# Sparse attention, soft mixture of experts and a gated feed-forward on one core: the order of the late expert weight loads

## The chip, the core and the metric

The kernel runs on one core of a Trainium2 chip. The metric is the time on the device in microseconds, from one launch. The arithmetic is done in float32, on TensorE (PE) in several passes; VectorE (DVE), ScalarE (ACT) and GpSimd (POOL) do the rest, and SyncE (SP) issues nearly all DMAs.

## What is computed

Three layers follow each other. First attention with 4 batches, 8 heads, 576 positions and 64 features a head; half the heads see the last 32 positions, half every 32nd position. Its output, 2304 tokens of 512, goes through a soft mixture of 8 experts with 4 slots each, and that through a gated feed-forward with 1536 hidden features.

```python
scores = scale * q @ k.T                      # masked: local for heads 0-3, strided for 4-7
x = softmax(scores) @ v                       # -> [2304, 512]
logits = x @ phi                              # [2304, 32]
d = softmax(logits, axis=0);  c = softmax(logits, axis=1)
slot_input = (d.T @ x).reshape(8, 4, 512)
for e in range(8):                            # w1[e] 512x1024, w2[e] 1024x512
    slot_out[e] = relu(slot_input[e] @ w1[e]) @ w2[e]
x = c @ slot_out.reshape(32, 512)
out = (silu(x @ w_gate) * (x @ w_val)) @ w_out
```

## The kernel before

**Stages.** A loop over 16 units (a pair of batches and a head) does the attention: scores (`qk`), exponentials (`expo`), transposes (`tr`) and the product with the values (`pv`). Beside it the outputs of pairs of heads (`x` tiles, six buffers of one tag) are transposed into `xT` (one buffer), multiplied with phi (`logits`, line 354), and summed into the expert slots (`slot`, line 421) with the transposed exponentials `eT`. After the last unit the softmax over tokens is finished (`weights_a`, `weights_b`, `slot_in`), and the slots' inputs stand in `sz`. Then the first expert product runs over 16 weights of one megabyte (`w1_mm`, line 623, in the order of `W1ORDER`: 1 to 6, 0, 7, 14, 8, 15, 9, 10, 13, 12, 11), then the second over another 16, numbered 16 to 31 (line 712, in the order of `W2ORDER`: the even ones, then the odd ones), and then the feed-forward, whose weights are converted on the chip tile by tile; its output products (line 819) fill the second half of the time.

**Expert weights and their memory.** SP loads the weights in halves of 512 KB; `loads` is the list of (weight, half) in the order of issue, and `load_half(k)` issues the next k of them. The order is written out by hand and interleaved with the units by `WSCHED`. SP is one queue that works in order: an issue whose memory is still in use holds up all that stand behind it. Fifteen buffers of two halves (pool `wp`) are filled during the attention, three of them first with feed-forward weights (`PRE`), whose memory 16, 18 and 20 take over once they are converted. 22, 24 and 26 have buffers of their own (pool `wp2`, with `sz` beside them) in the memory of the pool `ld`, where keys, values and masks lie; it is closed in step 16, after the last `pv`. Weights 0, 14 and 15 (`SPEC`) lie in the memory of attention outputs: their halves are called `wx` and take five of the six `x` buffers in turn, as their last readers (the `slot` matmuls) are done, and one half takes `xT`, whose last readers are the last `logits` matmuls. Weight 13 (`SPLIT`) has one half in the exponentials' tile `tmp` and one in `eT`. 28 and what follows take the buffers of weights 1 to 10 as `w1_mm` lets them go; each `w1_mm` of a weight that is not one of the four special ones calls `load_half(2)`.

**The order before.** After 20 the list reads: (0,0), 22, 24, 26 (six halves), (13,0), (0,1), (14,0), (14,1), (15,0), (15,1), (13,1), 28 and on. Half (0,0) is issued in step 15 or 16 by the `+ 1` of lines 605 and 613, into the `x` buffer that the `slot` call of step 18 (first batch pair, second output) reads last. (0,1) goes into `xT`.

Of the kernel before, what the change touches and what calls it, by code (L numbers as in the profile page):

```python
# [9 lines left out]
F32 = mybir.dt.float32  # L10
# [16 lines left out]
NB = 15  # L27
NB2 = 3
SPEC = (0, 14, 15)
W2ORDER = tuple(range(16, 32, 2)) + tuple(range(17, 32, 2))  # L30
SPLIT = 13
WORDER = list(range(1, 13)) + list(W2ORDER[:6]) + list(SPEC) + [SPLIT] + list(W2ORDER[6:])
W1ORDER = (1, 2, 3, 4, 5, 6, 0, 7, 14, 8, 15, 9, 10, 13, 12, 11)
PRE = [("g", 0), ("g", 1), ("o", 0)]
# [23 lines left out]
WSCHED = [2] + [2] * 16  # L58
# [53 lines left out]
def build(ctx: ExitStack, tc: tile.TileContext, cst, phi, kq, vh, w1, w2, wgv, wo, out):  # L112
# [13 lines left out]
    ap_ = es_att.enter_context(tc.tile_pool(name="att", bufs=1))  # L126
# [24 lines left out]

    wsrc = [w1[j] for j in range(16)] + [w2[j] for j in range(16)]
    loads = [(j, hf) for j in PRE + WORDER for hf in range(2)]
    loads.remove((SPEC[0], 0))
    loads.insert(2 * (NB + len(PRE)), (SPEC[0], 0))
    loads.remove((SPLIT, 0))
    loads.insert(2 * (NB + len(PRE) + NB2) + 1, (SPLIT, 0))
    wt, gt = {}, {}
    wn = [0]
    NW = len(loads)  # L160

    def load_half(k, pool=wp, bufs=NB):
        for _ in range(k):
            if wn[0] >= NW:
                return
            j, hf = loads[wn[0]]
            if j in SPEC:
                wt[j, hf] = (ap_.tile([128, 1024], F32, tag="xT", name="wx", bufs=1) if hf and j == SPEC[0] else
                             ap_.tile([128, 1024], F32, tag="x", name="wx", bufs=6))
            elif j == SPLIT:  # L170
                wt[j, hf] = ap_.tile([128, 1024], F32, tag="eT", name="wx", bufs=1) if hf else tmp[:, 0:1024]
            elif hf == 0:
                a = pool.tile([128, 2048], F32, tag="w", name="w", bufs=bufs)
                if j in PRE:
                    gt[j] = a.bitcast(I32)
                wt[j, 0], wt[j, 1] = a[:, 0:1024], a[:, 1024:2048]
            if j in PRE:
                o, i = wt[j, hf].bitcast(I32), (wgv if j[0] == "g" else wo)[j[1], hf].bitcast(I32)
            else:
                o, i = wt[j, hf], wsrc[j][hf]  # L180
            SP.dma_start(out=o, in_=i)
            wn[0] += 1
# [65 lines left out]
    def load_qk(u):  # L248
        if u >= 16:
            return  # L250
        SP.dma_start(out=kt[u % NQK][:, PAD:], in_=kq[u])

    def load_v(u):
        if u >= 16:
            return
        t = vt[u % NV]
        SP.dma_start(out=t[W - 64:W], in_=vh[u])
        t4 = t.rearrange("p (b i d) -> p b i d", b=2, i=NT)
        for i0, i1 in ((1, 3), (3, 6), (6, 9)):
            POOL.tensor_copy(t4[0:W - 64, :, i0:i1, :], t4[64:W, :, i0 - 1:i1 - 1, :])  # L260
# [10 lines left out]
    def qk(u):  # L271
        y = UNITS[u][1] // 4
        e = etile(u)
        q, k = qbd[u % NQK], kt[u % NQK]
        mx = mxs[u] = ap_.tile([128, NT], F32, tag="mx", name="mx", bufs=2)
        for i0, i1 in zip(CUT, CUT[1:]):
            ps = bank("sc", 2)
            for i in range(i0, i1):
                c0 = 64 * i
                for b in range(2):  # L280
                    h = slice(64 * b, 64 * b + 64)
                    PE.matmul(out=ps[h, W * (i - i0):W * (i - i0) + W], lhsT=q[h, 64 * i:64 * i + 64],  # L282
                              rhs=k[h, c0:c0 + W], start=True, stop=True, skip_group_check=True)
            p3 = ps[:, 0:(i1 - i0) * W].rearrange("p (j k) -> p j k", k=W)
            m3 = ms[:, i0:i1] if y else ml[:, i0:i1] if i0 == 0 else ml[:, 1:1 + i1 - i0]
            DVE.scalar_tensor_tensor(out=e[:, i0:i1], in0=p3, scalar=0.125, in1=m3, op0=ALU.mult, op1=ALU.add)  # L286
            DVE.tensor_reduce(out=mx[:, i0:i1], in_=e[:, i0:i1], axis=AX, op=ALU.max, negate=True)  # L287

    def expo(u, k):
        e, mx = etile(u), mxs[u]  # L290
        for i in range(CUT[k], CUT[k + 1]):
            ACT.activation(out=e[:, i], in_=e[:, i], func=AF.Exp, scale=1.0, bias=mx[:, i:i + 1])  # L292

    def tr(u):
        e = etile(u)
        for t in range(3):
            ps = bank("tr", 3)
            for j in range(3):
                PE.transpose(ps[0:W, 128 * j:128 * j + 128], e[:, 3 * t + j], ident)  # L299
            ACT.copy(attile[0:W, 3 * t:3 * t + 3], ps[0:W, 0:384].rearrange("p (j q) -> p j q", j=3))  # L300

    def pv(u):
        bp, h = UNITS[u]
        y = h // 4
        st, e = divmod(h % 4, 2)
        if e == 0:
            xt[bp, y, st] = ap_.tile([128, NT, 128], F32, tag="x", name="x", bufs=6)
        x, v = xt[bp, y, st], vt[u % NV]
        dn = ap_.tile([128, 2, NT, 1], F32, tag="dn", name="dn", bufs=2)
        half = []  # L310
        for i0, i1 in zip(CUT, CUT[1:]):
            ps = bank("pv", 2)
            for i in range(i0, i1):
                for b in range(2):
                    PE.matmul(out=ps[64 * b:64 * b + 64, 65 * (i - i0):65 * (i - i0) + 65], lhsT=attile[0:W, i, 64 * b:64 * b + 64],  # L315
                              rhs=v[0:W, 65 * (NT * b + i):65 * (NT * b + i) + 65], start=True, stop=True, skip_group_check=True)
            p3 = ps[:, 0:65 * (i1 - i0)].rearrange("p (j d) -> p j d", d=65)
            DVE.tensor_scalar_add(dn[:, 0, i0:i1], p3[:, :, HD:HD + 1], 1.0e-9)
            half.append((i0, i1, p3))
        DVE.reciprocal(dn[:, 1], dn[:, 0])  # L320
        for i0, i1, p3 in half:
            DVE.tensor_tensor(out=x[:, i0:i1, 64 * e:64 * e + 64], in0=p3[:, :, 0:HD],
                              in1=dn[:, 1, i0:i1].to_broadcast([128, i1 - i0, HD]), op=ALU.mult)

    xT = {}
# [167 lines left out]
    with tc.manual_schedule():  # L493
# [11 lines left out]
        load_qk(1)  # L505
        SP.dma_start(out=phi_t, in_=phi.rearrange("p (c s) -> p c s", c=4))
        load_half(WSCHED[0])
        load_v(1)
        load_qk(2)
# [43 lines left out]
        for p in range(8):  # L553
            bp, y, st = p // 4, p % 2, p // 2 % 2
            n = 2 * p + 3
# [30 lines left out]
        n = 0  # L586
        while n < 16 or any(k >= n for k in late):
            if n < 16:
                qk(n)
                load_qk(n + NQK)  # L590
            if 0 <= n - 1 < 16:
                tr(n - 1)
            if n < 16:
                expo(n, 0)
            for fn, a in side.pop(n, []):
                fn(*a)
            if n < 16:
                expo(n, 1)
            for fn, a in mid_.pop(n, []):
                fn(*a)  # L600
            if 0 <= n - 1 < 16:
                pv(n - 1)
                load_v(n + 1)
                if n == 16:
                    load_half(2 * (NB + len(PRE)) + 1 - wn[0])
                    es_ld.close()
                    wp2 = es_w2.enter_context(tc.tile_pool(name="wp2", bufs=NB2, side="right",
                                                           reuse_waits="tile"))
                    load_half(2 * NB2, wp2, NB2)
                    szt.append(wp2.tile([128, 4, 288], F32, name="sz", bufs=1))  # L610
                    POOL.memset(szt[0], 0.0)
            if n < 16:
                load_half(min(WSCHED[n + 1], 2 * (NB + (len(PRE) if n > 13 else 0)) + (n > 14) - wn[0]))
            for fn, a in late.pop(n, []) + first_.pop(n, []):
                fn(*a)
            n += 1
# [92 lines left out]
        for n, j in enumerate(W2ORDER):  # L709
            e, hf = divmod(j - 16, 2)  # L710
# [269 lines left out]
```

## Time and profile before

| | us |
|---|---|
| median of 3 runs | 359.76 |
| the 3 runs | 358.86, 359.76, 360.13 |
| the profiled execution | 358.82 |
| its span, first to last instruction | 356.9 |

| engine | busy us | share of the span | instructions |
|---|---|---|---|
| PE, matmuls | 337.2 | 94% | 2860 |
| PE, weight loads | 247.3 | 69% | 2860 |
| DVE | 236.4 | 66% | 485 |
| ACT | 194.7 | 55% | 462 |
| POOL | 140.9 | 39% | 147 |

Busy time of PE is that of pipelined matmuls, so 94% does not say that it runs at its peak. "SPq", "PEq" and the like are an engine's sequencer: waits and issues, in which the engine itself does nothing. "PEld" is the loading of the stationary operand. An arrow out<-in names the tile written and the tile or tensor read, L181 is line 181 of the kernel, and a name behind an arrow in brackets is what ended the idle time before. The attention takes the time up to about 100 us, the expert products that from 108 to 147 us, the feed-forward the rest.

### The profile page before, as it was taken

To read this page: it belongs to the slowest core of one execution; us is meant where nothing else is said; L and a number is where in the kernel's file an instruction comes from. 1 tells how busy PE (TensorE), PEld (TensorE's weight loads), DVE (VectorE), ACT (ScalarE), POOL (GpSimd) and SP (SyncE) were. 2 spreads that over 40 slices of the span, in tenths; PEclk is the share of its full clock that TensorE was granted. 3 is DMA by queue.
4 is the path that set the end of the run, shared out by engine and by line. 5 is a ranking of instruction groups with operands and counts; after the bars stand their busy time and mean duration, and the time that the engine had idled before them with its cause. 6 is when DMAs were issued, how large, how long until landed. Compare 5 with 4: busy or idle time off the path is not lost.

```text
span 356.9 us, 7428 instructions
## 1 busy us (share of the span) xinstructions
PE 337.2 (94%) x2860; PEld 247.3 (69%) x2860; DVE 236.4 (66%) x485; ACT 194.7 (55%) x462; POOL 140.9 (39%) x147
## 2 busy tenths in 40 slices
PE   8999998998799999979998999999998999999995
PEld 4788887897574243347785766876776788888885
DVE  4999889788360054396987998999778824252442
ACT  1997988978430023347766556456456445353441
POOL 2233323212100200226575768438368654334431
PEclk9999999999999999978999999999999999999999
DMA  7999999966679999933332433333300003030331
GB/s 288 409 407 407 391 378 388 376 220 242 241 290 416 408 411 406 409 139 115 118 119 85 150 119 118 118 120 118 118 1 2 1 0 119 0 118 2 119 116 62
DMA packets 20804, 71.94 MB, mean 202 GB/s; under 512 B 2336, under 2 KB 2720, under 8 KB 20768
## 3 DMA queue, kind: packets, MB, share of 16 engines
q1 hardware_dynamic: 20624, 71.45, 52.8%
q8 instruction: 23, 0.38, 0.4%
q14 instruction: 13, 0.11, 0.1%
q10 hardware_dynamic: 144, 0.01, 0.0%
HBM read 66.73 MB, written 4.72 MB: 200 GB/s over the span
## 4 chain that ended last, share of the span: by engine, by line
PE 53%; DVE 16%; DMA 12%; ACT 7%; POOL 6%; issue 5%; DVEq 0%; POOLq 0%; ACTq 0%
PE o L819 31%; DMA w<-in_w 9%; ACT tmp L292 4%; DMA wx<-in_w 3%; PE gv L792 3%; PE pv L315 3%; PE sc L282 3%; PE gv L793 3%; POOL hl L801 2%; DVE mx L287 2%; PE tr L299 2%; POOL wol L763 2%; DVE h L799 2%; DVE tmp L286 2%; DVE wg L224 2%
## 5 line engine op out<-in xcount | busy, mean ns | idle before, releaser
L801 POOL TENSOR_TENSOR hl<-h,hh 128x512 fp32r<-128x512 f32 (+1 forms) x60 | 72.2, 1205 | 90.7 <-ACT hh L800 90.6
L819 PE MATMUL o<-woh,hh 128*128 128x512 f32 (+1 forms) x222 | 86.8, 392 | 0.2 <-DVE acc L844 0.2
L819 PE MATMUL o<-wol,hh 128*128 128x512 f32 (+1 forms) x222 | 86.0, 390 | 0.0
L799 DVE TENSOR_TENSOR h<-gv,sg 128x512 f32<-128x512 f32 (+1 forms) x59 | 37.5, 636 | 55.7 <-ACT sg L798 42.4
L819 PE MATMUL o<-woh,hl 128*128 128x512 f32 (+1 forms) x222 | 66.7, 390 | 0.6 <-POOL hl L801 0.4
L800 ACT CAST hh<-h 128x512 fp32r<-128x512 f32 (+1 forms) x60 | 34.7, 578 | 54.8 <-DVE h L799 54.8
L819 PEld LDWEIGHTS o<-woh,hh 128*128 128x128 f32 x222 | 42.3, 190 | 10.0 <-DVE acc L844 0.6
L819 PEld LDWEIGHTS o<-woh,hl 128*128 128x128 f32 x222 | 41.8, 190 | 10.4 <-POOL hl L801 1.9
L260 POOL COPY v<-v 32x390 f32<-32x390 f32 (+1 forms) x48 | 23.9, 530 | 61.4 <-DMA v<-in_vh 52.0
L819 PEld LDWEIGHTS o<-wol,hh 128*128 128x128 f32 x222 | 42.3, 191 | 8.4
L292 ACT ACTIVATE tmp<-tmp,mx 128x96 f32<-128x96 f32 x144 | 40.0, 362 | 10.0 <-DVE mx L287 9.9
L798 ACT ACTIVATE sg<-gv 128x512 f32<-128x512 f32 (+1 forms) x60 | 33.4, 557 | 20.2 <-PE gv L792 19.3
L282 PE MATMUL sc<-k 64*64 64x96 f32 x576 | 27.8, 246 | 0.4 <-issue 0.2
L792 PE MATMUL gv<-cs,St 128*128 128x512 f32 (+1 forms) x60 | 25.7, 429 | 1.9 <-DVE St L781 1.9
L282 PEld LDWEIGHTS sc<-k 64*64 64x64 f32 x576 | 24.4, 133 | 3.0 <-issue 1.7
L763 POOL TENSOR_TENSOR wol<-wo,woh 128x512 fp32r<-128x512 f32 x12 | 15.3, 1289 | 23.3 <-ACT woh L760 23.3
L315 PEld LDWEIGHTS pv<-v,tmp 96*64 96x64 f32 x576 | 19.3, 137 | 6.4 <-ACT tmp L300 6.1
L315 PE MATMUL pv<-v,tmp 96*64 96x65 f32 x576 | 21.3, 225 | 1.9 <-ACT tmp L300 1.8
L300 ACT COPY tmp<-tr 96x384 f32<-96x384 f32 x48 | 19.7, 477 | 4.9 <-PE tr L299 4.8
L793 PE MATMUL gv<-cs,St 128*128 128x512 f32 (+1 forms) x59 | 22.4, 379 | 0.0
L299 PE MATMUL tr<-cst_t,tmp 128*96 128x128 f32 x144 | 19.9, 280 | 2.3 <-ACT xT L334 2.2
L220 DVE SCALAR_TENSOR_TENSOR cv<-g,cv 128x512 int32<-128x512 int32 x30 | 20.8, 693 | 0.6
(159 smaller groups left out, 484.9 us busy)
## 6 DMA issues: line engine op xcount, KB each, us to landing
w<-in_w SPq DMA_DIRECT2D x56, 512.0 KB, 7.7
g<-in_wgv SPq DMA_DIRECT2D x10, 1024.0 KB, 4.9
k<-in_kq SPq DMA_DIRECT2D x16, 576.0 KB, 7.5
g<-in_wo SPq DMA_DIRECT2D x5, 1024.0 KB, 4.8
v<-in_vh SPq DMA_DIRECT2D x16, 292.5 KB, 5.5
out<-osb SPq DMA_DIRECT2D x17, 256.0 KB, 2.1
wx<-in_w SPq DMA_DIRECT2D x7, 512.0 KB, 10.1
w<-in_wgv SPq DMA_DIRECT2D x4, 512.0 KB, 7.0
```

Source lines behind the costliest of these rows:

```text
L260: POOL.tensor_copy(t4[0:W - 64, :, i0:i1, :], t4[64:W, :, i0 - 1:i1 - 1, :])
L282: PE.matmul(out=ps[h, W * (i - i0):W * (i - i0) + W], lhsT=q[h, 64 * i:64 * i + 64], rhs=k[h, c0:c0 + W], start=True, stop=True, skip_grou ...
L292: ACT.activation(out=e[:, i], in_=e[:, i], func=AF.Exp, scale=1.0, bias=mx[:, i:i + 1])
L299: PE.transpose(ps[0:W, 128 * j:128 * j + 128], e[:, 3 * t + j], ident)
L315: PE.matmul(out=ps[64 * b:64 * b + 64, 65 * (i - i0):65 * (i - i0) + 65], lhsT=attile[0:W, i, 64 * b:64 * b + 64], rhs=v[0:W, 65 * (NT * b ...
L792: PE.matmul(out=pg[:, 0:n], lhsT=St[f][:, 0:128], rhs=csf[:, t0:t0 + n], start=True, stop=True)
L793: PE.matmul(out=pvv[:, 0:n], lhsT=St[f][:, 128:256], rhs=csf[:, t0:t0 + n], start=True, stop=True)
L798: ACT.activation(out=sg[:, 0:n], in_=pg[:, 0:n], func=AF.Silu)
L799: DVE.tensor_tensor(out=h[:, 0:n], in0=pvv[:, 0:n], in1=sg[:, 0:n], op=ALU.mult)
L800: ACT.copy(hh[bi, f][:, 0:n], h[:, 0:n])
L801: POOL.tensor_tensor(out=hl[bi, f][:, 0:n], in0=h[:, 0:n], in1=hh[bi, f][:, 0:n].bitcast(F32), op=ALU.subtract)
L819: PE.matmul(out=o[:, 0:c], lhsT=(a, a, l)[i][:, 128 * t:128 * t + 128], rhs=(woh, wol, woh)[i][f][:, c * k:c * k + c], start=(first and i ...
```

## The change

In the list of loads (0,0) is no longer moved ahead of 22; it stays ahead of (0,1), behind (13,0). The list after 20 then reads: 22, 24, 26 (six halves), (13,0), (0,0), (0,1), (14,0), (14,1), (15,0), (15,1), (13,1), 28 and on. (0,0) goes into `xT` and (0,1) into the `x` buffer, the other way round than before. Two counts of `load_half` lose the one half that was issued ahead. The other calls keep their counts, so that from (13,0) on each call reaches one half less far in the list; (13,1) is issued by the first `w1_mm`.

```diff
     loads = [(j, hf) for j in PRE + WORDER for hf in range(2)]
-    loads.remove((SPEC[0], 0))
-    loads.insert(2 * (NB + len(PRE)), (SPEC[0], 0))
     loads.remove((SPLIT, 0))
-    loads.insert(2 * (NB + len(PRE) + NB2) + 1, (SPLIT, 0))
+    loads.insert(2 * (NB + len(PRE) + NB2), (SPLIT, 0))
@@
-                wt[j, hf] = (ap_.tile([128, 1024], F32, tag="xT", name="wx", bufs=1) if hf and j == SPEC[0] else
+                wt[j, hf] = (ap_.tile([128, 1024], F32, tag="xT", name="wx", bufs=1) if not hf and j == SPEC[0] else
                              ap_.tile([128, 1024], F32, tag="x", name="wx", bufs=6))
@@
                 if n == 16:
-                    load_half(2 * (NB + len(PRE)) + 1 - wn[0])
+                    load_half(2 * (NB + len(PRE)) - wn[0])
                     es_ld.close()
@@
             if n < 16:
-                load_half(min(WSCHED[n + 1], 2 * (NB + (len(PRE) if n > 13 else 0)) + (n > 14) - wn[0]))
+                load_half(min(WSCHED[n + 1], 2 * (NB + (len(PRE) if n > 13 else 0)) - wn[0]))
```

## Rows read from the trace of the kernel before

**Rows 1.** The page's 40 slices of 8.9 us: granted clock, bytes moved.

```profile
PEclk9999999999999999978999999999999999999999
GB/s 288 409 407 407 391 378 388 376 220 242 241 290 416 408 411 406 409 139 115 118 119 85 150 119 118 118 120 118 118 1 2 1 0 119 0 118 2 119 116 62
```

**Rows 2.** Chain that ended last, in order of time, 86 to 162: start, us, what.

```profile
103.69 11.67 DMA wx<-in_w
...
125.58 10.38 DMA w<-in_w
...
135.97 10.23 DMA w<-in_w
...
146.25 1.08 PE pv L712 x4
```

**Rows 3.** Timeline of SP, 83 to 112: start, us, engine, line, operation, count.

```profile
83.73 7.50 SPq L181 DMA_DIRECT2D w<-in_w  x6
98.77 0.33 SPq L181 DMA_DIRECT2D wx<-in_w  x1
99.14 2.97 SPq L181 DMA_DIRECT2D w<-in_w  x6
...
103.09 7.62 SPq L181 DMA_DIRECT2D wx<-in_w  x6
```

**Rows 4.** Waits of SP, 91.5 to 99.1: total us, times, longest.

```profile
SPq L181 <- PE tr L421: 7.5, 1, 7.5
```

**Rows 5.** Line 181, the two issues at 90.42 and 90.79: time to landing.

```profile
DMA to landing us min/median/max: 4.6/5.9/7.1
```

**Rows 6.** Line 181, the one issue at 98.77: time to landing.

```profile
DMA to landing us min/median/max: 3.5/3.5/3.5
```

**Rows 7.** Busy us by stretch: PE, PEld, DVE, ACT, POOL, clock, DMA share, GB/s.

```profile
90.00:92.00 2.00, 2.00 (x29) 1.17 (x29) 0.36 (x1) 1.66 (x5) 0.00 (x0) 1.00 1.01 377
...
96.00:98.00 2.00, 2.00 (x32) 1.54 (x32) 0.92 (x4) 0.23 (x1) 0.00 (x0) 1.00 0.04 10
...
102.00:104.00 2.00, 2.00 (x33) 1.77 (x34) 1.43 (x6) 0.88 (x3) 0.00 (x0) 1.00 0.92 309
...
112.00:116.00 4.00, 4.00 (x40) 1.41 (x31) 0.00 (x0) 0.00 (x0) 0.00 (x0) 1.00 1.02 414
```

**Rows 8.** Timeline of PE's weight loads, 107 to 150: idle before and releaser in brackets.

```profile
116.68 0.12 PEld L623 LDWEIGHTS sc<-wx,sz 128*32 128x32 f32 x3 [1.14 <-DMA wx<-in_w]
...
119.26 0.12 PEld L623 LDWEIGHTS sc<-wx,sz 128*32 128x32 f32 x3 [1.16 <-DMA wx<-in_w]
...
130.51 0.13 PEld L712 LDWEIGHTS pv<-w,hz 128*32 128x32 f32 x4 [0.30 <-issue]
...
143.68 0.14 PEld L712 LDWEIGHTS pv<-w,hz 128*32 128x32 f32 x4 [0.51 <-DMA w<-in_w]
144.96 0.14 PEld L712 LDWEIGHTS pv<-w,hz 128*32 128x32 f32 x4 [1.13 <-DMA w<-in_w]
146.24 0.14 PEld L712 LDWEIGHTS pv<-w,hz 128*32 128x32 f32 x4 [1.14 <-DMA w<-in_w]
```

**Rows 9.** Timeline of POOL, 80 to 150.

```profile
93.03 1.06 POOL L611 MEMSET sz<- 128x1152 f32 x1 [5.20 <-PE pv L315]
```

**Rows 10.** Timeline of PE's matmuls, 76 to 160.

```profile
95.56 1.06 PE L354 MATMUL lg<-xT,phi_t 128*32 128x288 f32 x8 [0.35 <-ACT xT L334]
...
108.49 5.69 PE L623 MATMUL sc<-w,sz 128*32 128x512 f32 x47
```

**Rows 11.** Line 653, the one issue at 137.31: time to landing.

```profile
DMA to landing us min/median/max: 11.5/11.5/11.5
```

**Rows 12.** Timeline of ACT, 104 to 166.

```profile
150.29 1.25 ACT L198 ACTIVATE wg<-g 128x512 f32<-128x512 f32 x2
```

**Rows 13.** Busy us by stretch, columns as in rows 7.

```profile
152.00:156.00 4.00, 2.07 (x8) 1.04 (x7) 3.81 (x7) 1.07 (x3) 0.00 (x0) 0.97 0.69 271
156.00:160.00 4.00, 3.87 (x8) 2.19 (x8) 3.39 (x7) 2.23 (x4) 2.42 (x2) 0.50 0.00 0
```

## What the change does to the time: the prediction

> **What bounds the kernel now.** I read the slices first. The weight loads run at over 400 GB/s for long stretches, but between slices 8 and 11 the rate falls to 220 to 290 GB/s, before it is over 400 again [rows 1]. The question is whether that hole costs anything, so the chain of waits comes next. From 103.7 us to 146.2 us it holds DMAs alone: one expert half after another, each 10.2 to 11.7 us from issue to landing, and only then the last four matmuls of the second expert product (line 712) at 146.25 [rows 2]. So the end of the expert stage is set by when the last weight half lands, and that goes back to when the queue was fed.
>
> The timeline of SP shows where it was not fed. Six halves are issued from 83.73 on and the last of them is out at 91.23 (83.73 + 7.50). The next issue is at 98.77 [rows 3]. In between SP stands for 7.5 us in one wait, which PE's line 421 ends, the token-slot matmuls of the first batch pair [rows 4]. By the kernel's list of loads this is half (0,0): it goes into the third buffer of attention outputs, and those matmuls are its last reader. Behind it stand the six halves of 22, 24 and 26, which have nothing to do with that buffer. The DMA engines drain what is queued and then idle: 377 GB/s in 90 to 92 us, 10 GB/s in 96 to 98, 309 still in 102 to 104, then 414 [rows 7].
>
> The rest of the question is who would notice earlier weights. PE's weight loads tell it: a group of four column matmuls follows the next with 0.30 us of idle on that unit when nothing is late, and five groups have more, put down to DMA: 1.14 and 1.16 us in the first expert product, 0.51, 1.13 and 1.14 us in the second [rows 8]. Everywhere else PE runs through at its own pace, although the chain says DMA; most of the wait in the chain is beside PE work. So what earlier loads can return is bounded by these five waits.
>
> **The change, part by part.** No DMA, matmul or byte is added or taken away: 34 halves from 22's first to 31's last are issued in another order, and the two halves of weight 0 swap memory, the first into the transposed activations' tile (xT), the second into the buffer of outputs. Instruction counts on every engine stay. SP's own cost is 0.33 to 0.50 us an issue: 2.97 us for six [rows 3], unchanged.
>
> *The moved halves on SP.* After 91.23 comes 22. Its memory, and 24's and 26's, is that of the keys, values and masks. The trace has an operation with the same release: the memset of sz, in the same pool beside them, starts at 93.03, let go by PE's line 315, the last product with the values [rows 9]. So even if all six halves wait for all of that memory they leave from 93.0 on; if each waits for its own part alone, from 91.3. I take 91.3 to 93.0; neither end matters, since the halves issued at 90.4 and 90.8 land only 4.6 and 7.1 us after issue, at 95.1 and 97.9 [rows 5], so that the engines still have work, and a half into an empty queue needs 3.5 us from issue to landing [rows 6].
>
> *What is queued behind, and its waits.* Half (13,0) needs the exponentials' tile, read before that line-315 product. (0,0) now waits for xT, whose last readers are the logits matmuls, 95.56 + 1.06 = 96.6 us [rows 10]. (0,1) and (14,0) wait for what (0,0) waits for now, 98.77 [rows 3]. (14,1) follows the release that starts the chain at 103.69 [rows 2]. (15,1) and (13,1) wait for the last slot matmuls and 28 for the first expert matmuls, which start at 108.49 [rows 10]; at 0.43 us a group of four (0.13 of load and 0.30 idle [rows 8]) and two groups a weight, the first is read by about 109.4. None of these uncovers the engines: a half is 0.524 MB, at 414 GB/s [rows 7] 1.27 us, and ten halves are issuable by 99.2, so they carry the engines from 95.1 or 97.9 to 107.8 or 110.6. At 103.7 two more are let go, at about 107.7 another two, and 28 would have to land at 95.1 + 16 x 1.28 = 115.6 or later: from 109.4 it has over 6 us, with 3.5 needed [rows 6].
>
> *When the last half lands.* One hop of the chain is eight halves, in 10.23 us, or 1.28 us each [rows 2]. From the landing of the half before 22: early end, it lands 1.28 after 95.1 as the rate asks, 96.4 + 34 x 1.28 = 139.9; late end, 97.9 + 43.5 = 141.4, and with the 1.7 us that the present stretch loses on the same pace (the half of 98.77 lands at 102.3 [rows 3, 6], 33 halves later it is 146.2 and not 144.5) 143.1. Now it is 135.97 + 10.23 = 146.2 [rows 2]. The queue gains 3.1 to 6.3 us; I take 5, between the ends, since the loss of 1.7 came with the restart, which is gone.
>
> *What PE makes of it.* The five waits above, less 0.30 each: 0.84 + 0.86 + 0.21 + 0.83 + 0.84 = 3.58 us [rows 8]. The first two belong to weights 14 and 15, which would be wanted at 116.68 - 0.84 = 115.8 and at 119.26 - 0.84 - 0.86 = 117.6; they would land by 112.0 and 114.5 in the later case (11 and 13 halves after 97.9). The last three need 31's second half by 146.24 - 3.58 = 142.7. At 139.9 or 141.4 it is there; at 143.1 it is 0.4 late. So the return is 3.2 to 3.6 us, I take 3.6, and 1.4 us of the 5 is lost beside PE. Past 142.7 each microsecond of lateness is one microsecond of the result.
>
> *What comes after.* The second product's result, the softmax pieces and the memset of hz hang on PE's own progress here and move with it. The last stage reads its first converted tile from a load behind the weights: issued at 137.31, landed 11.5 us later at 148.8, first read by ACT at 150.29 [rows 11, 12]. It follows the weights on SP and comes forward by the same 3 to 6 us, so it stays ahead of a reader that comes forward by 3.6. From there the kernel is PE work of fixed size: its end comes forward whole. Nothing in the attention part ahead of 91 us is touched.
>
> A rule of the Trainium skill speaks against this much: "DMA: Bandwidth & Descriptors", section Specifications, gives an HBM limit of about 358 GB/s for a core. As an estimate, by that 34 halves would take 49.8 us and the last would land at 146.2 to 147.7, no earlier than now, and the time would stay. The trace disagrees: 414 GB/s in the stretch itself [rows 7]; I weigh slower supply below by rows alone.
>
> **The sum.** The profiled execution took 358.82 us, with a span of 356.9 and 1.9 around it. 358.82 - 3.6 = 355.2. It is 0.94 under the median of the three runs, 359.76; the same step from the median gives 356.1, which is the forecast.
>
> **The rivals.** *Supply too slow.* If the halves come at 377 GB/s, the rate of 90 to 92 us [rows 7], a half takes 1.39 us and 34 take 47.3: the last lands at 143.7 to 145.2, and PE is 1.0 to 2.5 us late on it. The gain is 1.1 to 2.6, the time 357.2 to 358.7; I put it at 357.7. For it speaks that the stretch of 100 to 107 is slow now; against it that 108 to 146 is not.
>
> *The change does not do what it says.* 22 could find a wait as long as the old one (a release of the whole pool that is tied to something near 98.8). The time stays at 359.8. Against it stands the memset at 93.03 [rows 9].
>
> *The clock spares the start of the last stage.* The granted clock is 0.50 in 156 to 160 us [rows 13], the lower level of 1.2 GHz, after 4 us in which PE was busy for 2.07; the slices show 7 and 8 tenths there [rows 1], 2 to 3 tenths and 1 to 2 tenths of 8.9 us lost, 2.7 to 4.5 us of full-clock time. Part of that is idle anyway. If earlier, denser work keeps the clock up, 1 to 3 us more come back: 353.1 to 355.1, say 354.1. Against it: the idle time before the fall lies behind the weights and moves with them, unchanged.
>
> *Slower: the clock falls again.* The same fall once or twice more on the matmuls of line 819, which have no slack, costs 2.7 to 4.5 us each. It decides against the change once more than 3.6 + 1.1 = 4.7 us are lost, so with two falls: 356.1 + 5.4 to 9 = 361.5 to 365. The place would be just behind the present fall, where PE still waits for tiles that are converted. For it speaks only that one fall is there already. The Trainium skill ("TensorE: Matmul & The Clock Gate", section "What's actually happening") says that the throttled state is the default and activity releases it; by that rule fewer waits of PE make a further fall less likely. No row shows a second one.
>
> **How the numbers follow.** Forecast 0.66 (355.5 to 356.8 with the term's ends and the runs' spread), slow supply 0.13, clock spared 0.08, no effect 0.08, slower 0.05. 0.3%, about what a measurement of this kernel can tell from no change, is 1.1 us. Faster by more: 0.66 + 0.13 + 0.08, less a little of the slow-supply end, 0.86; within: 0.09; slower: 0.05. The range takes in the spared clock's middle and slow supply's: 353.9 to 358.1, and leaves out about 0.17.
>
> **What would show each step.** SP's wait on line 421 gone or under 3 us, and 22's halves issued by 94; no slice window with 10 GB/s in 94 to 100 us; last expert half landed by 143; no idle above 0.5 us put down to DMA on PE's weight loads in lines 623 and 712; the first expert matmul still near 108.5, the second product's end near 143.7 and everything behind it shifted alike, half clock included. The prediction is wrong if 22 still waits, if the first expert matmul moves, or if the stage behind 150 us does not shift with the weights.

## The result: 355.5 us after 359.8, and the profile after

| | before | after |
|---|---|---|
| median of 7 runs, us | 359.76 | 355.52 |
| lowest and highest, us | 357.46, 362.15 | 353.83, 356.55 |
| the profiled execution, us | 358.82 | 356.04 |
| its span, us | 356.9 | 354.3 |

The ratio is 0.988, with a 95% interval from 0.984 to 0.992: 4.2 us less, 2.8 to 5.7 by the interval. The forecast was 356.1.

The slices of the page after, granted clock and bytes moved:

```profile
PEclk9999999899999999969999999999999999999999
GB/s 287 408 409 401 385 397 393 361 189 221 355 409 410 407 411 407 386 71 82 118 120 118 118 120 126 111 123 116 118 1 2 1 0 120 0 118 2 120 118 61
```

And its chain of waits, shares of the span by engine, first before and then after:

```profile
PE 53%; DVE 16%; DMA 12%; ACT 7%; POOL 6%; issue 5%; DVEq 0%; POOLq 0%; ACTq 0%
```

```profile
PE 67%; DVE 14%; POOL 6%; ACT 5%; issue 5%; DMA 2%; DVEq 0%; POOLq 0%; ACTq 0%; SPq 0%
```

The hole of the transfers is two slices long instead of four: 355 and 409 GB/s in slices 10 and 11, counted from 0, where there were 241 and 290 [rows 1]. The other two, slices 8 and 9 (71 to 89 us), lie ahead of SP's 7.5 us wait and are as low as before, 189 and 221; the prediction read all four as one hole, but the change touches the second half of it alone. DMA has 2% of the chain where it had 12%. SP's timeline (start, us, operation, count):

```profile
85.26 12.90 SPq L179 DMA_DIRECT2D w<-in_w  x12
98.26 0.38 SPq L179 DMA_DIRECT2D tmp<-in_w  x1
99.34 10.74 SPq L179 DMA_DIRECT2D wx<-in_w  x7
```

Its waits from 91 to 107 us (total, times, longest):

```profile
SPq L179 <- DVE wo L222: 3.8, 1, 3.8
SPq L179 <- DMA w<-in_w: 3.3, 4, 0.9
SPq L179 <- PE pv L419: 2.6, 1, 2.6
SPq L179 <- PE pv L313: 0.8, 1, 0.8
```

Twelve halves now leave in one run instead of six [rows 3], and no wait of 7.5 us stands among them [rows 4]. The one of 3.8 us, for feed-forward weights to be converted, is ahead of the six moved halves; the kernel before has it too, with 4.1 us. The transfers answer in the same stretches as in rows 7 (the columns are those too):

```profile
96.00:98.00 2.00, 1.65 (x15) 0.81 (x13) 0.00 (x0) 1.25 (x3) 0.00 (x0) 1.00 0.93 344
...
102.00:104.00 2.00, 2.00 (x23) 1.32 (x23) 1.63 (x5) 1.32 (x5) 0.00 (x0) 1.00 1.03 420
```

344 GB/s instead of 10, and 420 instead of 309. In the chain of waits, in order of time, nearly all is PE's own work up to 137.3 us, where DMAs stood from 103.7 to 146.2 [rows 2], and behind it stands one DMA that loads for the feed-forward:

```profile
110.11 14.30 PE sc L621 x127
...
129.92 7.00 PE pv L710 x64
...
137.42 8.32 DMA g<-in_wgv
...
145.79 2.50 POOL wol L761 x2
```

The same step of POOL in the chain before:

```profile
148.32 2.49 POOL wol L763 x2
```

That DMA is the 2%, and it sets nothing. The chain names it as what let POOL go at 145.79, 0.55 us behind the load with which the next step begins (145.24, below). In the kernel before POOL starts the same 0.55 us behind that load (148.32 - 147.77), let go by ACT; and in the run below without weight 31, where the first load for the feed-forward lands at 141.5 (136.27 + 5.2), it is 0.55 us again (145.08 - 144.53).

And on PE's weight loads the late groups of rows 8 are gone; the last of both products, and the load with which the next step begins:

```profile
110.04 0.14 PEld L621 LDWEIGHTS sc<-w,sz 128*32 128x32 f32 x4
...
142.82 0.16 PEld L710 LDWEIGHTS pv<-w,hz 128*32 128x32 f32 x8
143.28 0.13 PEld L710 LDWEIGHTS pv<-w,hz 128*32 128x32 f32 x4 [0.30 <-issue]
143.70 0.13 PEld L710 LDWEIGHTS pv<-w,hz 128*32 128x32 f32 x4 [0.30 <-issue]
...
145.24 0.98 PEld L733 LDWEIGHTS sc<-cst_t,so 128*128 128x128 f32 x8 [0.24 <-ACT so L724]
```

Where there were 1.13 and 1.14 us of idle "put down to DMA" there are now 0.30 us of the ordinary pace.

For what follows I use one length, which I call the expert stage: from the first weight load of the first product to the load with which the step behind the second begins. After, that is 145.24 - 110.04 = 35.20 us. In the kernel before the first product starts at 108.48 (its first matmul is 108.49 [rows 10]) and the step behind it here:

```profile
147.77 0.98 PEld L735 LDWEIGHTS sc<-cst_t,so 128*128 128x128 f32 x8 [0.22 <-ACT so L726]
```

That is 39.29 us. The stage is 4.1 us shorter, about as much as the medians differ. The two spans differ by 2.6 only, because the attention of the profiled execution after took 1.6 us longer; that is not the change, as the last section shows.

### The profile page after: what moved, and what is told of

It is laid out like the page before. It is cut to its first block, busy times and chain, and to the rows that moved or that the text cites. A ratio compares the mean times of both kernels' runs of the same rounds, so it can differ in the third digit from the quotient of the medians.

```text
span 354.3 us, 7429 instructions
## 1 busy us (share of the span) xinstructions
PE 335.5 (95%) x2860; PEld 250.0 (71%) x2860; DVE 236.4 (67%) x485; ACT 195.4 (55%) x462; POOL 140.2 (40%) x147
## 4 chain that ended last, share of the span: by engine, by line
PE 67%; DVE 14%; POOL 6%; ACT 5%; issue 5%; DMA 2%; DVEq 0%; POOLq 0%; ACTq 0%; SPq 0%
PE o L817 32%; PE sc L621 4%; PE pv L313 4%; PE sc L280 4%; PE gv L790 3%; PE tr L297 3%; PE pv L710 3%; PE gv L791 3%; POOL hl L799 2%; DMA g<-in_wgv 2%; ACT tmp L290 2%; POOL wol L761 2%; DVE h L797 2%; PE tr L489 2%; PE tr L331 2%
## 5 line engine op out<-in xcount | busy, mean ns | idle before, releaser
L280 PE MATMUL sc<-k 64*64 64x96 f32 x576 | 28.7, 251 | 0.7 <-issue 0.5
L280 PEld LDWEIGHTS sc<-k 64*64 64x64 f32 x576 | 25.4, 137 | 3.8 <-issue 1.6
```

## The experiments

The theory: SP's stand at one half (the 7.5 us in which it waits and issues nothing) held back six others that wait for nothing; the transfers made good for it only at the end of the second product, and PE waited for them. With the stand filled PE itself sets the end of the stage, so more transfer time buys nothing further. Rivals: the two swapped places give the gain; the transfers still set the end; the clock gives it. The stage is read from one profile of each run, the ratio from all its executions.

| run | ratio to before, 95% interval | expert stage in its profile, us |
|---|---|---|
| before | 1 | 39.29 |
| changed kernel | 0.988 (0.984 to 0.992) | 35.20 |
| changed kernel again | 0.986 (0.983 to 0.989) | 35.19 |
| order alone | 0.984 (0.981 to 0.988) | 35.19 |
| places alone | 0.999 (0.996 to 1.001) | 40.23 |
| two halves ahead | 0.992 (0.989 to 0.995) | 36.77 |
| four halves ahead | 0.990 (0.987 to 0.994) | 35.63 |
| changed, weight 31 not loaded | 0.989 (0.985 to 0.993) | 35.20 |
| before, weight 31 not loaded | 0.995 (0.992 to 0.998) | 37.69 |

**Order alone.** The changed kernel with the old places of weight 0's two halves.

```diff
+    i0 = loads.index((SPEC[0], 0))
+    loads[i0], loads[i0 + 1] = loads[i0 + 1], loads[i0]
@@
-    wt[j, hf] = (... tag="xT" ... if not hf and j == SPEC[0] else
+    wt[j, hf] = (... tag="xT" ... if hf and j == SPEC[0] else
```

> The changed order with the old places: 22, 24, 26 are issued ahead of both halves of weight 0, but its second half still lies in xT and its first in the output buffer, so the list runs (13,0), (0,1), (0,0). Theory (the gain is SP's 7.5 us stand that no longer holds back the six halves): ratio to before 0.988 to 0.990, like the changed kernel, the six halves issued by about 94 to 98, no weight-load wait for DMA in the first and second expert product. Rival (the swap of the two places gives the gain, or a part of it): ratio nearer to 1.

Measured: 0.984, and the changed kernel's stage. The ratio is a little better than forecast, but its interval reaches to 0.988 and overlaps the changed kernel's. SP's timeline has the run of twelve:

```profile
84.24 11.86 SPq L181 DMA_DIRECT2D w<-in_w  x12
```

The chain of waits, in order of time, is PE's own pace through both products:

```profile
109.07 14.30 PE sc L623 x127
...
141.85 1.90 PE pv L712 x16
```

**Places alone.** The kernel before with the halves' roles exchanged: the second half of weight 0 in the output buffer and ahead of 22, the first in xT.

```diff
-    loads.remove((SPEC[0], 0))
-    loads.insert(2 * (NB + len(PRE)), (SPEC[0], 0))
+    loads.remove((SPEC[0], 1))
+    loads.insert(2 * (NB + len(PRE)), (SPEC[0], 1))
@@
-    wt[j, hf] = (... tag="xT" ... if hf and j == SPEC[0] else
+    wt[j, hf] = (... tag="xT" ... if not hf and j == SPEC[0] else
```

> The old order with the new places: the second half of weight 0 goes into the output buffer and stands ahead of 22, as the first half did; the first half goes into xT. Theory: SP again stands some 7.5 us at that half, ratio 0.997 to 1.003, five late groups of weight loads as before. Rival (the places matter): ratio 0.988 to 0.993.

Measured: 0.999, no change. SP's timeline has the old stand:

```profile
84.60 7.49 SPq L181 DMA_DIRECT2D w<-in_w  x6
99.64 0.33 SPq L181 DMA_DIRECT2D wx<-in_w  x1
```

Its wait from 91 to 110 us:

```profile
SPq L181 <- PE tr L421: 7.5, 1, 7.5
```

And PE's weight loads are late at the end of the second product, as before:

```profile
146.79 0.14 PEld L712 LDWEIGHTS pv<-w,hz 128*32 128x32 f32 x4 [1.14 <-DMA w<-in_w]
148.06 0.14 PEld L712 LDWEIGHTS pv<-w,hz 128*32 128x32 f32 x4 [1.12 <-DMA w<-in_w]
```

The profiled execution is the slowest of its twelve (361.01 us), and its stage is 0.9 us longer than before, which the median does not show. A wait for weight 0's first half, which is issued behind the stand here, comes on top in its first product, so the late groups are six and not the expected five:

```profile
116.11 0.16 PEld L623 LDWEIGHTS sc<-wx,sz 128*32 128x32 f32 x8 [1.87 <-DMA wx<-in_w]
```

The two together settle it: the order is the whole gain. The swap of memory adds nothing that shows, since the order alone has the same stage without it.

**Two halves ahead.** The kernel before with (0,0) behind 22 instead of ahead of it.

```diff
-    loads.insert(2 * (NB + len(PRE)), (SPEC[0], 0))
+    loads.insert(2 * (NB + len(PRE)) + 2, (SPEC[0], 0))
@@
-    load_half(2 * (NB + len(PRE)) + 1 - wn[0])
+    load_half(2 * (NB + len(PRE)) - wn[0])
@@
-    load_half(2 * NB2, wp2, NB2)
+    load_half(2 * NB2 + 1, wp2, NB2)
@@
-    load_half(min(WSCHED[n + 1], 2 * (NB + (len(PRE) if n > 13 else 0)) + (n > 14) - wn[0]))
+    load_half(min(WSCHED[n + 1], 2 * (NB + (len(PRE) if n > 13 else 0)) - wn[0]))
```

> The kernel before with only the two halves of 22 ahead of (0,0), 24 and 26 behind it as before. Theory: the queue gains 2 x 1.28 = 2.6 us of work for its stand, so the last half lands some 2.6 us earlier than 146.2 for the same start of the first product; PE's wait falls by about that, of 4.1 to about 1.5 us: ratio 0.992 to 0.994. Rival (transfers start late in any case and only the whole reordering helps): ratio 1. Rival (the gain of the changed kernel lies in the clock, not in the loads): ratio without relation to the number of halves.

Measured: 0.992, and a stage of 36.77 us, 1.6 above the changed kernel's where 1.5 were expected. SP still stands, but behind eight halves, as its timeline has it:

```profile
85.25 8.44 SPq L181 DMA_DIRECT2D w<-in_w  x8
100.28 0.33 SPq L181 DMA_DIRECT2D wx<-in_w  x1
```

Two groups of weight loads are late where there were five:

```profile
143.96 0.14 PEld L712 LDWEIGHTS pv<-w,hz 128*32 128x32 f32 x4 [1.02 <-DMA w<-in_w]
145.25 0.14 PEld L712 LDWEIGHTS pv<-w,hz 128*32 128x32 f32 x4 [1.15 <-DMA w<-in_w]
```

**Four halves ahead.** The same with (0,0) behind 24 (+ 4 in place of + 2).

> The kernel before with the halves of 22 and 24 ahead of (0,0), 26 behind it. Theory: 5.1 us more work for the stand; the last half lands about 141 to 143 for a start of the first product at 108.5, PE's five waits for DMA are gone or under 0.5 us in all, and the ratio is that of the changed kernel, 0.986 to 0.989: the step from two halves to four gives the rest, and the step from four to six nothing. Rival (each half ahead gives its share, because the transfers still set the end): ratio 0.990 to 0.992 here, with a rest that only six halves give.

Measured: 0.990, in the rival's range, with an interval that reaches into the theory's, so the time does not decide. The profile says more: the stage is 35.63 us, 0.4 above the changed kernel's. SP's timeline:

```profile
83.40 10.23 SPq L181 DMA_DIRECT2D w<-in_w  x10
```

PE's last weight loads; the group before the last is split in two:

```profile
141.40 0.12 PEld L712 LDWEIGHTS pv<-w,hz 128*32 128x32 f32 x2 [0.30 <-issue]
141.82 0.12 PEld L712 LDWEIGHTS pv<-w,hz 128*32 128x32 f32 x2 [0.31 <-issue]
142.27 0.14 PEld L712 LDWEIGHTS pv<-w,hz 128*32 128x32 f32 x4 [0.33 <-DMA w<-in_w]
```

The idle of 0.33 us hides the wait. Where nothing is late four loads go at once, then the next four 0.42 us later (143.28 and 143.70 in the changed kernel). Here two go, then two, and the last four at 142.27, just behind the landing of weight 31's second half (issued at 132.03, landed 10.2 us later, at 142.2). That is one step of 0.42 to 0.45 us more, which is what the stage is longer by. So with four halves ahead the transfers still set the end, by 0.4 us, as the rival had it; only with six does PE.

The first two halves take 2.5 us off the stage, the next two 1.1, the last two 0.4. The last half lands 37.7, 35.2, 34.1 and 32.9 us after the stage's start with none, two, four and six halves ahead, so only the first pair brings about the 2.6 us that a pair was priced at, the others 1.1 each, and of the last 1.1 PE had 0.4 to take. Neither expectation has this: the rival's equal shares are not there, and "nothing" for the last pair was too strong.

**Weight 31 not loaded, in the changed kernel and in the one before.** The two halves are left out of the list, and the last four matmuls of the second product read weight 29 again: PE does the same work, one megabyte less is moved.

```diff
+    loads = [(j, hf) for j, hf in loads if j != W2ORDER[-1]]
@@
-    rhs=wch(j, k)
+    rhs=wch(j if n < 15 else W2ORDER[-2], k)
```

> The changed kernel without the load of weight 31; its matmuls read weight 29 instead, so one megabyte less is loaded and PE's work is the same. Theory (PE sets the end of the expert products now): ratio like the changed kernel's, within 0.002. Rival (the transfers still set it): 2.6 us faster than the changed kernel, ratio 0.979 to 0.981.

> The kernel before without the load of weight 31; its matmuls read weight 29 instead. Theory (in the kernel before the transfers set the end of the second product, while the two waits in the first product stay): the last two of the three late groups of the second product come on time, 1.7 us less, ratio 0.994 to 0.9965, and the two late groups of the first product stay. Rival (the loads did not hold the kernel before, the clock did): ratio 1.

Measured: in the changed kernel 0.989, no better than with weight 31 loaded, with an interval that leaves out the rival's 0.979 to 0.981, and a stage of 35.20 us, the same to the hundredth. Its chain goes through PE to the end:

```profile
142.18 1.90 PE pv L711 x16
```

SP's timeline has its last expert weights out by 129.1 (124.98 + 4.12), where the changed kernel issues the last one at 132.77:

```profile
124.98 4.12 SPq L180 DMA_DIRECT2D w<-in_w  x4
```

In the kernel before it is 0.995, and the stage falls by 1.6 us (1.7 expected): the two late groups of the first product stay (with one more of 0.61 us of idle in this execution), the last two of the second are gone. PE's weight loads:

```profile
117.38 0.12 PEld L624 LDWEIGHTS sc<-wx,sz 128*32 128x32 f32 x3 [1.15 <-DMA wx<-in_w]
119.94 0.12 PEld L624 LDWEIGHTS sc<-wx,sz 128*32 128x32 f32 x3 [1.14 <-DMA wx<-in_w]
...
144.21 0.14 PEld L713 LDWEIGHTS pv<-w,hz 128*32 128x32 f32 x6 [0.35 <-DMA w<-in_w]
```

So a megabyte less is worth 1.6 us where transfers set the end and nothing where PE does. That the changed kernel's stage is not set by its last loads is shown by this pair, not argued; no other late group is left on its weight loads.

The third rival, the clock, has no part in the stage: its granted share is 1.00 from 108 to 148 us before and from 110 to 146 us after.

**The changed kernel again**, beside the others:

> The changed kernel once more, beside the others on the same chip. Theory: ratio 0.988 to 0.990. Between profiles the start of the first expert product may differ with the granted clock in the attention; from that start to the end of the second product 34.6 us, as in the changed kernel, where before had 38.8.

Measured: 0.986, with a stage of 35.19 us. To the end of the product's last matmul it is 34.7 us (140.69 + 1.92 - 107.91), where 34.6 was expected.

## Why the prediction was right, step by step

*The stand and its end* came as forecast. 22 was put between 91.3 and 93.0; its halves left at 92.9 and 93.3, in an execution whose attention ran 1.6 us late, so at the early end: each weight waits for its own part of the old memory. 24 has the wait of 0.8 us on the last product with the values (line 313 after).

*The new waits* are there and cost nothing: 2.6 us before (14,1) and 2.8 before (15,1), between the issues at 106.1 and 109.3. The transfers kept their rate behind them, 420 GB/s in 102 to 104.

*The last half* was to land 3.1 to 6.3 us earlier, 5 as the value taken. It is issued at 132.77 and lands 10.2 us later, 32.9 us after the stage's start; before that was 146.2 - 108.5 = 37.7. That is 4.8.

*PE's five waits* were to give 3.58 us and gave 4.1. The first product's length, up to the load of the step behind it (line 696, at 124.55 before; line 694, at 124.34 after), went from 16.07 to 14.30, 1.77 where the terms made 1.70. The second half of the stage went from 23.22 to 20.90, 2.3 where they made 1.88. The mis-sized term is the third, 0.51 - 0.30 = 0.21 us. The 0.30 is the pace between groups that follow matmuls of their own kind; this group comes right behind transposes, and there the loads of two groups run together, as the row of 142.82 after shows (eight in 0.16 us). So all of 143.68 - 143.03 = 0.65 us was wait, 0.44 more than the term, of the missing 0.5. The row of 143.03 in the timeline before, which has four loads where after has eight:

```profile
143.03 0.14 PEld L712 LDWEIGHTS pv<-w,hz 128*32 128x32 f32 x4
```

*The margin* behind it is thinner than forecast: of the 4.8 us by which the last half lands earlier 4.1 return, so 0.7 are unused, where the prediction had 1.4. With four halves ahead instead of six it is used up: the last half lands 1.1 us later there, and the stage is 0.4 longer.

*The start* moved, which the prediction had named as a sign against it: the first expert matmul was to stay near 108.5 and stood at 110.0 in the profiled execution. In the second profile of the same kernel it stood at 107.9. What moved it lies ahead of every load that changed places: the run of weight loads starts at 85.26 where it started at 83.73 [rows 3], so 1.5 of the 1.6 us were lost by then, and the last section shows where.

*What comes behind* moved whole. From the stage's end to the end of the program it was 209.2 us before and 209.0 after. One reason given was wrong: the first load for the feed-forward was to come forward with the weights by 3 to 6 us. It waits for memory that PE lets go, in each of the six profiles with two halves or more moved ahead 26.94 us after the stage's start; here it left at 136.98, no more than 0.3 us earlier on the clock of the trace and 1.9 earlier against the stage's start. It lands sooner all the same, since less stands in the queue ahead of it, 8.5 us after issue instead of 11.5 [rows 11], at 145.5 (5.2 us after issue where weight 31 is not loaded). Its time to landing in the changed kernel (line 651, the issue at 136.98):

```profile
DMA to landing us min/median/max: 8.5/8.5/8.5
```

ACT, its first reader, by its timeline:

```profile
147.76 1.24 ACT L196 ACTIVATE wg<-g 128x512 f32<-128x512 f32 x2
```

So 2.2 us of cover are left where there were 1.5.

*The rivals.* Slow supply did not come: the halves came at 404 to 420 GB/s in the stretches from 98 to 116 us. The 358 GB/s of the Trainium skill's page "DMA: Bandwidth & Descriptors" (section Specifications) do not hold for this core's stream, before or after; the row gets them by dividing a stack's 716 GB/s by two cores, and this program runs on one. The half clock at the start of the last stage stayed, and the second fall behind it did not come:

```profile
153.00:156.00 3.00, 2.70 (x5) 1.28 (x6) 2.39 (x5) 1.48 (x3) 1.29 (x1) 0.50 0.00 0
156.00:160.00 4.00, 4.00 (x10) 3.13 (x11) 2.70 (x5) 3.00 (x6) 2.58 (x2) 0.52 0.49 147
```

The rival of a spared clock is not idle, though: this fall lasts about 6.8 us in both profiles of the changed kernel, in the one before and with places alone, and 3.4 us in the other five profiles (154.2 to 157.6 in order alone). What lies behind the stage takes 209.0 to 209.6 us in the four and 208.1 to 208.8 in the five. Either order of the loads is found in both groups, so the order alone does not decide it; what does is not shown.

## What to carry to other kernels

A DMA queue that works in order is read by its longest wait: what stands behind it, whether that needs the same release, and whether the transfer engines run dry in the meantime. Price the cure not by the stand (7.5 us here) nor by how much earlier the last transfer lands (4.8), but by the waits of the reader that go (4.1), each against the pace the reader has at that very place and not by the idle printed before one load (0.33 for a wait of 0.4 with four halves ahead); what the reader does not wait for is a margin and nothing more. If a megabyte taken out of the end of the loads changes nothing, they no longer set the end of the stage, and its next gain has to come from elsewhere.

## What the runs showed that was not expected

The granted clock of PE falls to half in the attention in some executions and not in others of the same program, and that moves the whole rest. In the profiled execution of the changed kernel 64 to 68 us has a mean of 0.57, behind four microseconds in which PE was busy for 2.34. In its second profile the same stretch is at full clock, and PE was busy for 2.45 of the four microseconds ahead of it. First the two stretches of the one (columns as in rows 7):

```profile
60.00:64.00 4.00, 2.34 (x45) 2.01 (x44) 3.80 (x9) 3.33 (x11) 0.58 (x2) 1.00 1.04 400
64.00:68.00 4.00, 4.00 (x43) 3.67 (x44) 3.49 (x13) 3.29 (x10) 1.13 (x3) 0.57 0.98 374
```

Then those of the other:

```profile
60.00:64.00 4.00, 2.45 (x47) 2.12 (x45) 3.79 (x10) 3.94 (x14) 0.85 (x3) 1.00 1.01 390
64.00:68.00 4.00, 4.00 (x61) 2.83 (x59) 3.89 (x11) 3.89 (x12) 0.54 (x3) 1.00 0.97 374
```

The first matmuls of the first product in the second profile, by PE's timeline:

```profile
107.91 4.50 PE L621 MATMUL sc<-w,sz 128*32 128x512 f32 x38
```

The expert stage starts at 110.04 in the one and at 107.91 in the other: 2.1 us between two executions of one kernel, half of what the change brings. Order alone and two halves ahead show the fall as well; before, places alone, four halves ahead and both kernels without weight 31 do not. In the changed kernel without weight 31 PE was busy for 2.23 us of the same four and the clock stayed. So these busy times do not tell what decides it, and no run here was made to find out. A span of one profile against that of another would have given 2.6 us for this change; the length of the stage that the change touches gives 35.19 or 35.20 in every profile that has the full reordering.
